# Range checks of the weights at chunk boundaries, LayerNorm's high part straight from x, and sums with high parts first, in a two-layer attention and FFT-filter kernel

## The chip, the cores and the metric

The kernel runs on one core of a Trainium2 chip. Its engines are TensorE (PE; its weight loads are shown apart as PEld), VectorE (DVE), ScalarE (ACT), GpSimd (POOL) and SyncE (SP, which issues most DMAs). The metric is the device time of one execution in microseconds (us); the median of several runs counts.

## The reference

x is 2048 x 1024 in float32; the model has two layers, each an attention with 32 heads of 32 and a filter in the frequency domain, all with the same weights.

```python
def _A_ref(x, wqkv, wo):
    qkv = (x @ wqkv).reshape(B, S, 3, H, Dh).transpose(2, 0, 3, 1, 4)
    q, k, v = qkv[0], qkv[1], qkv[2]
    p = softmax(einsum("bhqd,bhkd->bhqk", q, k) * Dh ** -0.5, axis=-1)
    o = einsum("bhqk,bhkd->bhqd", p, v)
    return o.transpose(0, 2, 1, 3).reshape(B, S, D) @ wo

def _B_ref(x, w_r, w_i):
    X = rfft2(x, axes=(-2, -1)) * (w_r + 1j * w_i)
    return irfft2(X, s=(S, D), axes=(-2, -1))

for _ in range(2):
    x = x + _A_ref(_layernorm(x), wqkv, wo)
    x = x + _B_ref(_layernorm(x), w_r, w_i)
```

## The kernel before

**Numbers as two halves.** A float32 operand of a large matmul is split into a float16 high part and a float16 rest (`split`: ScalarE writes the high part, L167, VectorE the rest, L168), and a product is three matmuls: high by high, high by rest, rest by high. This holds only in a range of values, so the kernel gathers range checks: the largest magnitude of wqkv, of wo and of the filter's weights, the smallest variance and the largest reciprocal of a softmax sum. `combine_flags` makes one number of them at the end (L1126 to L1156), and if it is set, a slower general path computes everything again. With the inputs given it is not set. The weights are the same in both layers, and the maxima are taken in the first one.

**Stages of one layer.**
1. *Head.* `ln` normalises 16 tiles of 128 rows. For a tile, ScalarE writes xn = (x − mean) · r (L315) and then its high part `hl` (L167), VectorE writes the rest, and SP issues two transposing DMAs (L320) that put both parts into the buffer `big`. The sums for V (`v_tiles`, L382) and for q and k (`qk_chunk`, L338) of the first head group follow. ScalarE and VectorE carry each finished sum out of PSUM (`R<-x`, `R<-o`).
2. *Attention loop.* Eight groups `g` of four heads, four chunks `c` of 512 queries, sixteen tiles `kt` of 128 keys. For each (g, c, kt) PE makes scores (`S`, L564), ScalarE exponentials (L568, 128x1024 each, two per tile), PE the products with V (`PV`, L574), and VectorE adds the exponentials up (`add`: the first two tiles in L585, the others in L587) into `acc`. A boundary is the passage from one chunk to the next: 31 in a loop. There `fin` adds `acc` over partitions with four matmuls by ones (the column sums, L593), takes reciprocals (L594 to L599) and scales the output (L600); `out` stores it. Between all this PE works off the q, k and V sums of later groups as filler (q and k sums L338, V sums L382), and `Weights.prep` loads and splits the weights for them, slice by slice of 128x512 (`wst`), three slices ahead.
3. *End of attention:* the product with wo (L440), and the residual.
4. *Filter.* Transposes and a first matmul (32 steps, L795, L804), a loop over 36 steps that works on 32 units (`fb` L864, `fc` L896 and the complex products L903 to L912, `binv` L864, `cinv` L933), then the inverse stage. `loadw` fetches one unit's weights, two units ahead; GpSimd flips signs in them (L848).

**Order of work.** PE and ScalarE follow the order of the code in the attention loop; the other engines, and all of them elsewhere, are ordered by the compiler's scheduler, which places each instruction when it expects it to be ready. Each engine runs its list strictly in order.

**Where the maxima are taken.** In the first layer `Weights.prep` reduces each slice behind its split (L259, 48 in all: 13 in the head, 35 in the loop); `absmax` loads wo a second time and reduces it in 16 pieces in the first filter stage (L789), and `loadw` reduces each unit's weights (L840, 32). L840 stands ahead of L848 and reads the tile that L848 rewrites.

At a chunk boundary the last pair of exponentials is added in two iterations, and `fin` runs in the second, kt = 1:

```python
                for w in late[:1]:
                    add(*w)
                    if w[2] == NKT - 1:
                        fin(*w[:2])
```

Of the kernel before, what the change touches and what calls it, by code (L numbers as in the profile page):

```python
# [115 lines left out]
def ln_scale(nc, sm, cst, mv, eng, n=1):  # L116
# [7 lines left out]
    eng.tensor_tensor(r, r, q, op=ALU.mult)  # L124
    return r
# [63 lines left out]
class AttnPools:  # L189
# [22 lines left out]
    def open_small(self):  # L212
        small = self.small = Pools(self.tc, "left")
        self.pp = small("at_p", 8)
        self.qp = small("at_q", 1)
# [11 lines left out]
class Weights:  # L227


    def __init__(self, nc, ap, wp, flag):  # L230
        self.nc, self.ap, self.wp, self.flag, self.W, self.n = nc, ap, wp, flag, {}, 0

    def prep(self, ph):
# [22 lines left out]
        for i, (h, l, _) in enumerate(sl):  # L256
            split(nc, h, l, st[i], SW)
            if self.flag is not None:
                nc.vector.tensor_reduce(self.flag.pop(), st[i], axis=AX.XY, op=ALU.max, apply_absolute_value=True)  # L259
            load()  # L260
            yield

# [5 lines left out]
def attention(nc, tc, layer, ap, xin, yd, wts, wo, cst, dram, flags):  # L268
# [29 lines left out]
    def ln(t0, n):  # L298
# [10 lines left out]
        r = ln_scale(nc, sm, cst, mv, nc.vector, n)  # L309
        b = sm.tile([128, n], F32, name=f"lb{n}")  # L310
        nc.vector.scalar_tensor_tensor(b, mv[:, 0::2], -1.0, r, op0=ALU.mult, op1=ALU.mult)
        for i in range(n):
            t = t0 + i
            xn = pp.tile([128, 1024], F32, name="xn", tag="p")
            nc.scalar.activation(xn, ap.x[:, t], AF.Identity, bias=b[:, i:i + 1], scale=r[:, i:i + 1])  # L315
            hl = pp.tile([128, 2, 1024], F16, name="hl", tag="p")
# [7 lines left out]
    def qk_chunk(ph, c):  # L324
# [11 lines left out]
        for d in range(8):  # L336
            for i, (a, b) in enumerate(((w[:, 0, d], xh[c][:, d]), (w[:, 0, d], xl[c][:, d]), (w[:, 1, d], xh[c][:, d]))):
                nc.tensor.matmul(ps, a, b, start=d == 0 and i == 0, stop=d == 7 and i == 2)  # L338
                if d < 7 or i < 2:
                    yield  # L340
# [29 lines left out]
    def v_tiles(ph, t2):  # L370
# [6 lines left out]
        for j in range(2):  # L377
            c, o = t2 // 2, (t2 % 2) * 256 + j * 128
            for d in range(8):
                a, b = xh[c][:, d, o:o + 128], xl[c][:, d, o:o + 128]  # L380
                for i, (l, r) in enumerate(((a, w[:, 0, d]), (a, w[:, 1, d]), (b, w[:, 0, d]))):
                    nc.tensor.matmul(ps[:, j], l, r, start=d == 0 and i == 0, stop=d == 7 and i == 2)  # L382
                    if (3 * d + i) % 2 and (j, d, i) != (1, 7, 2):
                        yield
# [165 lines left out]
    last_v = vk.pop()  # L550
    for v in vk:
        run(v)
# [28 lines left out]
    def add(g, c, kt):  # L581
        for hf in range(2):
# [3 lines left out]
            elif kt:  # L586
                nc.vector.tensor_add(acc[hf], acc[hf], p)  # L587
# [46 lines left out]
    with tc.manual_schedule(engines={mybir.EngineType.PE, mybir.EngineType.Activation}):  # L634
        for g in range(NG):
# [3 lines left out]
            for u in range(NCH * NKT):  # L639
# [4 lines left out]
                if kt % 2 == 0:  # L644
# [3 lines left out]
                    pend = []  # L648
                for w in late[:1]:
# [32 lines left out]
        run(wof)  # L682
    with tc.manual_schedule(engines={mybir.EngineType.PE}):
# [72 lines left out]
def spectral(nc, tc, ap, yd, xout, a, cst, fast, flags=None, nxt=None):  # L756
# [23 lines left out]
    wos = []  # L780

    def absmax(i):

        if flags is not None and 0 <= i < 16:
            s = p3.tile([128, 512], F32, name="wo")
            nc.sync.dma_start(s, a["wo"][(i // 2) * 128:(i // 2 + 1) * 128, (i % 2) * 512:(i % 2) * 512 + 512])
            wos.append(s)
        while len(wos) == 3 or (wos and i == 15):
# [453 lines left out]
```

## Time and profile before

| | us |
|---|---|
| median of 3 runs (lowest, highest) | 3838.1 (3837.19, 3840.38) |
| profiled execution, its own time | 3841.8 |
| span of the profiled execution | 3839.8 |

| stage, first layer / second layer | us |
|---|---|
| head, up to the first scores | 118.2 / 152.8 (with the inverse stage of the filter before it) |
| attention loop | 1508.7 / 1489.8 |
| end of attention | 47.8 / 47.9 |
| first filter stage | 49.1 / 48.8 |
| unit loop of the filter | 162.4 / 150.7 |
| inverse stage and stores, second layer | 63.6 |

The profile is of one execution. "Busy" is the time in which an engine executes an instruction; a group is all instructions of one line and shape. In a timeline a row begins with the start in us and a length; `x4` means four instructions in a row, and a bracket at the end tells how long the engine idled before it and what it then got. Names such as `R`, `big` or `wst` are buffers: `R<-R,p` is the sum of exponentials, `Q<-x,Q` the rest of a q sum, `wqk<-wst,wqk` the rest of a weight slice.

### The profile page before, as it was taken

The numbers are of one execution on the slowest core, as the hardware profiler recorded it, in microseconds if no ns is written. First come the engines' busy times: TensorE is split into PE (matmuls) and PEld (weight loads), VectorE is DVE, ScalarE is ACT, GpSimd is POOL, SyncE is SP. The second block draws the span as 40 slices with busy tenths as digits, with TensorE's granted clock in tenths as the row PEclk, the third lists the DMA queues.
The fourth block names the chain that finished last, engine by engine and source line by source line (L and its number), as shares of the span: only waits on it lengthen the run. The fifth ranks groups of instructions, "written<-read, shape, count | busy, mean of one in ns | idle before, by whom it ended". The sixth has DMA issues, their size and how long they took to land.

```text
span 3839.8 us, 79585 instructions
## 1 busy us (share of the span) xinstructions
PE 3713.6 (97%) x32951; PEld 1637.3 (43%) x32951; DVE 3165.3 (82%) x3869; ACT 2900.6 (76%) x3567; POOL 309.1 (8%) x386
## 2 busy tenths in 40 slices
PE   6999999999999999999989999999999999999998
PEld 4422433342234233378854334333423432333788
DVE  6789899889998988965666998899899889889554
ACT  4687887888788876667856888888888888666595
POOL 1000000000000000004320000000000000000143
PEclk9999999999999999999999999999999999999999
DMA  8000000000000221244270000000000002112433
GB/s 206 15 18 18 12 12 18 18 12 16 14 26 7 72 67 70 72 147 135 63 176 15 18 18 13 12 18 23 10 18 12 23 12 91 53 64 72 151 99 105
DMA packets 165573, 194.07 MB, mean 51 GB/s; under 512 B 74960, under 2 KB 120656, under 8 KB 164176
## 3 DMA queue, kind: packets, MB, share of 16 engines
q1 hardware_dynamic: 164912, 188.82, 16.0%
q8 instruction: 260, 4.26, 0.5%
q14 instruction: 113, 0.93, 0.1%
q10 hardware_dynamic: 288, 0.07, 0.0%
HBM read 123.83 MB, written 48.23 MB: 45 GB/s over the span
## 4 chain that ended last, share of the span: by engine, by line
PE 74%; DVE 11%; issue 8%; ACT 3%; DMA 2%; POOL 2%; SPq 0%; DVEq 0%; POOLq 0%; ACTq 0%
PE o L574 20%; PE s L564 17%; PE x L338 12%; PE x L382 7%; PE x L440 6%; DVE R L587 3%; PE s L440 2%; PE ps L864 2%; PE ps L804 2%; ACT p L568 1%; PE s L593 1%; PE ps L795 1%; PE ps L979 1%; DMA wst<-in_wp 1%; PE ps L933 1%
## 5 line engine op out<-in xcount | busy, mean ns | idle before, releaser
L568 ACT ACTIVATE p<-s,bias 128x1024 f32<-128x1024 f32 x2048 | 2169.8, 1112 | 553.6 <-PE s L564 536.7
L587 DVE TENSOR_TENSOR R<-R,p 128x1024 f32<-128x1024 f32 x1792 | 2084.4, 1217 | 109.0 <-ACT p L568 105.7
L574 PE MATMUL o<-p,R 128*32 128x512 f32 x8192 | 985.2, 598 | 0.0
L338 PE MATMUL x<-big,wqk 128*128 128x512 f16 x2880 | 679.2, 381 | 16.8 <-DVE R L168 7.6
L564 PEld LDWEIGHTS <-R 32*128 32x128 f16 x12288 | 231.2, 92 | 755.3 <-issue 639.8
L338 PEld LDWEIGHTS <-wqk 128*128 128x128 f16 x3072 | 276.9, 98 | 449.7 <-issue 163.0
L574 PEld LDWEIGHTS o<-p,R 128*32 128x32 f32 x8192 | 213.7, 109 | 524.1 <-issue 524.1
L564 PE MATMUL s<-R 32*128 32x512 f16 x6144 | 430.2, 378 | 6.7 <-ACT p L568 5.0
L564 PE MATMUL s<-Q,R 32*128 32x512 f16 x6144 | 425.7, 378 | 7.1 <-DVE R L481 5.5
L382 PE MATMUL x<-wv,big 128*128 128x256 f16 x2784 | 331.9, 276 | 35.4 <-DMA big<-hl 35.4
L382 PEld LDWEIGHTS <-big 128*128 128x128 f16 x3072 | 293.1, 99 | 147.3 <-issue 68.9
L585 DVE SCALAR_TENSOR_TENSOR R<-p 128x1024 f32<-128x1024 f32 x128 | 153.8, 1203 | 197.2 <-ACT p L568 196.8
L440 PE MATMUL x<-big 128*128 128x512 f16 x1050 | 241.6, 380 | 0.0
L363 POOL PARTITION_ALL_REDUCE mall<-mqk x16 | 43.0, 2684 | 2310.6 <-DVE mqk L357 2299.1
L440 PEld LDWEIGHTS <-big 128*128 128x128 f16 x1344 | 124.3, 98 | 180.6 <-issue 42.7
L912 DVE TENSOR_TENSOR H<-G,H 128x512 f16<-128x512 f32 (+1 forms) x68 | 46.3, 680 | 113.7 <-ACT H L911 113.6
L864 PE MATMUL ps<-cbi,H 128*128 128x256 f16 (+1 forms) x792 | 100.2, 275 | 7.6 <-ACT H L911 6.0
L857 ACT COPY U<-ps 64x256 f32<-64x256 f32 (+1 forms) x272 | 97.2, 357 | 10.9 <-PE ps L864 5.8
L857 ACT COPY B<-ps 64x256 f32<-64x256 f32 (+1 forms) x272 | 97.1, 357 | 7.0 <-PE ps L864 3.5
L864 PE MATMUL ps<-cb,big 128*128 128x256 f16 x780 | 97.2, 274 | 0.0
L167 ACT ACTIVATE R<-x 128x512 f16<-128x512 f32 x88 | 52.6, 598 | 53.4 <-PE x L338 53.3
L864 PEld LDWEIGHTS <-H 128*128 128x128 f16 (+1 forms) x792 | 76.6, 99 | 20.2 <-ACT H L911 7.1
(428 smaller groups left out, 2922.8 us busy)
## 6 DMA issues: line engine op xcount, KB each, us to landing
wst<-in_wp SPq DMA_DIRECT2D x96, 256.0 KB, 3.0
R<-y SPq DMA_DIRECT2D x32, 512.0 KB, 5.3
w<-in_w SPq DMA_DIRECT2D x60, 256.0 KB, 2.7
od<-ohl SPq DMA_DIRECT2D x56, 256.0 KB, 2.4
big<-od SPq DMA_DIRECT2D x16, 896.0 KB, 6.9
y<-R SPq DMA_DIRECT2D x20, 512.0 KB, 2.6
R<-in_x SPq DMA_DIRECT2D x16, 512.0 KB, 5.5
wst<-in_wo SPq DMA_DIRECT2D x32, 256.0 KB, 3.1
```

The lines of the kernel that those rows point to most:

```text
L167: nc.scalar.activation(hi, src, AF.Copy, scale=scale)
L338: nc.tensor.matmul(ps, a, b, start=d == 0 and i == 0, stop=d == 7 and i == 2)
L382: nc.tensor.matmul(ps[:, j], l, r, start=d == 0 and i == 0, stop=d == 7 and i == 2)
L440: nc.tensor.matmul(p, a, b, start=start and d == ds[0] and i == 0, stop=stop and d == ds[-1] and i == 2)
L564: nc.tensor.matmul(s[h // 2][:, h % 2], K[g][r, a, kt * 128:kt * 128 + 128], Q[g][r, b, c * 512:c * 512 + 512], start=i == 0, stop=i == 2)
L568: nc.scalar.activation(p, s[hf], AF.Exp, bias=bias[g], scale=SCALE / (SQ * SQ))
L574: nc.tensor.matmul(O[g, c][32 * h:32 * h + 32], V[g][:, kt, 32 * h:32 * h + 32], P[g, c, kt, h // 2][:, h % 2], start=kt == 0, stop=kt == ...
L585: nc.vector.scalar_tensor_tensor(acc[hf], P[g, c, 0, hf], 1e-34, p, op0=ALU.add, op1=ALU.add)
L587: nc.vector.tensor_add(acc[hf], acc[hf], p)
L804: nc.tensor.matmul(pa[:, j], tt[:, j], mm[:, g], start=True, stop=True)
L857: nc.scalar.copy(ov[64 * r:64 * r + 64, a0:a0 + m, x], tl[64 * x:64 * x + 64, :m, r])
L864: nc.tensor.matmul(out, l, r, start=k == 0, stop=k == len(mm_) - 1)
```

## The change

1. *Maxima.* The reduces L259, L789 and L840, and the second load of wo in L789's stage, go. A list `unseen` of pieces takes their place, and `look()` takes the maximum of one piece. In the first layer the pieces are the float16 high parts of split weights, 128x1024, 24 in all (five in the head, nineteen at boundaries). In the second layer they are the 17 pieces of the filter's weights and the 8 of wo, 128x1024 float32, loaded into a pool of two buffers one boundary ahead (`take`).
2. *Boundaries.* Both last adds, then `look`, then `fin` stand in iteration kt = 0.
3. *LayerNorm.* ScalarE writes the high part straight from x, with the factor 256 in r; xn is a second activation of x; the rest is a subtraction. The high part's transpose is issued ahead of the rest's.
4. *Sums.* A q, k or V sum takes its 16 matmuls with the high part of x first, then the 8 with the rest.
5. *Flags.* `combine_flags` runs in the unit loop of the second filter, at step 20, with PSUM tiles of that loop; only the load of the result stays at the end.
6. `dynamic_dma_scratch_size=4096` is passed to the compiler.

```diff
@@ Weights
         for i, (h, l, _) in enumerate(sl):
             split(nc, h, l, st[i], SW)
-            if self.flag is not None:
-                nc.vector.tensor_reduce(self.flag.pop(), st[i], axis=AX.XY, op=ALU.max, apply_absolute_value=True)
             load()
             yield
+        if self.flag is not None:
+            v = w[:, 0].rearrange("p d n -> p (d n)")
+            self.unseen += [(v[:, o:o + 1024], None) for o in range(0, 512 * len(sl), 1024)]
+
+    def take(self, i):
+        if len(self.unseen) > i and self.unseen[i][1] is not None:
+            src = self.unseen[i][1]
+            t = self.ap.lookp.tile([128, 1024], F32, name="look")[:, :src.shape[1]]
+            self.nc.sync.dma_start(t, src)
+            self.unseen[i] = (t, None)
+
+    def look(self):
+        if self.unseen:
+            self.take(0)
+            self.nc.vector.tensor_reduce(self.cols.pop(0), self.unseen.pop(0)[0], axis=AX.X, op=ALU.max,
+                                         apply_absolute_value=True)
+            self.take(0)
@@ ln
-            xn = pp.tile([128, 1024], F32, name="xn", tag="p")
-            nc.scalar.activation(xn, ap.x[:, t], AF.Identity, bias=b[:, i:i + 1], scale=r[:, i:i + 1])
             hl = pp.tile([128, 2, 1024], F16, name="hl", tag="p")
-            split(nc, hl[:, 0], hl[:, 1], xn, SX)
+            xn = pp.tile([128, 1024], F32, name="xn", tag="p")
             c, o = t // 4, (t % 4) * 128
-            for j, p in enumerate((xh, xl)):
-                nc.sync.dma_start(p[c][:, :, o:o + 128], hl[:, j], transpose=True)
+            for dst in (hl[:, 0], xn):
+                nc.scalar.activation(dst, ap.x[:, t], AF.Identity, bias=b[:, i:i + 1], scale=r[:, i:i + 1])
+            nc.sync.dma_start(xh[c][:, :, o:o + 128], hl[:, 0], transpose=True)
+            nc.vector.tensor_sub(hl[:, 1], xn, hl[:, 0])
+            nc.sync.dma_start(xl[c][:, :, o:o + 128], hl[:, 1], transpose=True)
@@ qk_chunk (v_tiles alike)
-        for d in range(8):
-            for i, (a, b) in enumerate(((w[:, 0, d], xh[c][:, d]), (w[:, 0, d], xl[c][:, d]), (w[:, 1, d], xh[c][:, d]))):
-                nc.tensor.matmul(ps, a, b, start=d == 0 and i == 0, stop=d == 7 and i == 2)
+        mms = [(w[:, i, d], xh[c][:, d]) for d in range(8) for i in range(2)] + [(w[:, 0, d], xl[c][:, d]) for d in range(8)]
+        for i, (a, b) in enumerate(mms):
+            nc.tensor.matmul(ps, a, b, start=i == 0, stop=i == 23)
@@ attention loop
+                    if kt == 0 and late:
+                        for w in late:
+                            last_add = add(*w)
+                        with tc.issue_after(last_add.ins):
+                            wts.look()
+                        done = [late[1][:2]]
+                        fin(*done[0])
+                        late = []
                 for w in late[:1]:
                     add(*w)
-                    if w[2] == NKT - 1:
-                        fin(*w[:2])
-                        done = [w[:2]]
@@ loadw
-        if flags is not None:
-            nc.vector.tensor_reduce(flags["wb"][:, i:i + 1], wt, axis=AX.X, op=ALU.max, apply_absolute_value=True)
@@ unit loop of the filter
+        if i == 20 and join:
+            join(ps)
@@ build
+        later = [a["w"][:, o:min(o + 1024, WOFF[-1])] for o in range(0, WOFF[-1], 1024)]
+        later += [a["wo"][128 * d:128 * d + 128, :] for d in range(8)]
```

How the engines' lists change is seen at three places. VectorE at the second boundary of the first layer, before; `zt<-s` reads the column sums, the two L585 begin the new chunk:

```order
L587 TENSOR_TENSOR R<-R,p 128x1024 x4
L585 SCALAR_TENSOR_TENSOR R<-p 128x1024
L594 STREAM_TRANSPOSE zt<-s 128x512
L585 SCALAR_TENSOR_TENSOR R<-p 128x1024
L596 RECIPROCAL rc<-zt 128x16
L597 TENSOR_TENSOR fr<-fr,rc 128x16
L599 STREAM_TRANSPOSE zt<-rc 128x512
L168 SCALAR_TENSOR_TENSOR Q<-x,Q 128x512
L600 SCALAR_TENSOR_TENSOR zt<-oc,zt 128x512
```

And after, at the same place (L613 is the old L587, L611 the old L585, L171 the old L168):

```order
L613 TENSOR_TENSOR R<-R,p 128x1024 x4
L281 TENSOR_REDUCE fw<-wqk 128x1
L621 STREAM_TRANSPOSE zt<-s 128x512
L623 RECIPROCAL rc<-zt 128x16
L624 TENSOR_TENSOR fr<-fr,rc 128x16
L626 STREAM_TRANSPOSE zt<-rc 128x512
L627 SCALAR_TENSOR_TENSOR zt<-oc,zt 128x512
L611 SCALAR_TENSOR_TENSOR R<-p 128x1024 x2
L171 SCALAR_TENSOR_TENSOR Q<-x,Q 128x512
```

PE at the same boundary, before and then after (L593 and L620 are the column sums, L564 and L590 scores, L600 the product with V, L338 filler; LDWEIGHTS loads a matmul's weights):

```order
L564 LDWEIGHTS R
L564 MATMUL s<-R 128x512
L593 MATMUL s<-R,ones 32x512 x4
L338 LDWEIGHTS wqk
L338 MATMUL x<-big,wqk 128x512
```

```order
L600 MATMUL o<-p,R 32x512 x8
L620 MATMUL s<-R,ones 32x512 x4
L590 LDWEIGHTS R
L590 MATMUL s<-R 128x512
L590 LDWEIGHTS R
```

The column sums have moved from behind the scores of kt = 1 to ahead of them. On VectorE the look stands behind the last add, and all of `fin` ahead of the first adds of the new chunk. Eight rows further on before, two reduces `fw<-wst` of the weight slices stood between the adds; they are gone. VectorE in the unit loop of the first filter, one unit before and after:

```order
L903 TENSOR_TENSOR G<-ps,w 128x256
L840 TENSOR_REDUCE fwb<-w 128x1
L904 TENSOR_TENSOR t__20768<-ps,w 128x256
L905 TENSOR_TENSOR G<-ps,w 128x256
L906 TENSOR_TENSOR t__20768<-ps,w 128x256
L912 TENSOR_TENSOR H<-G,H 128x2x256
```

```order
L922 TENSOR_TENSOR G<-ps,w 128x256
L923 TENSOR_TENSOR t__20609<-ps,w 128x256
L924 TENSOR_TENSOR G<-ps,w 128x256
L925 TENSOR_TENSOR t__20609<-ps,w 128x256
L931 TENSOR_TENSOR H<-G,H 128x2x256
```

Only the reduce is missing. ScalarE in the first head around the first sums of k and q, before; `R<-x` and `R<-o` carry them out of PSUM, the rest is LayerNorm:

```order
L167 ACTIVATE R_90<-x_471 128x512
L315 ACTIVATE xn_456<-R_90,lb2_454,r2_446 128x1024
L167 ACTIVATE hl_458<-xn_456 128x1024
L315 ACTIVATE xn_463<-R_90,lb2_454,r2_446 128x1024
L167 ACTIVATE hl_465<-xn_463 128x1024
L315 ACTIVATE xn_518<-R_90,lb2_516,r2_508 128x1024
L167 ACTIVATE R_90<-o_533 128x512
```

And after:

```order
L170 ACTIVATE R_92<-x_468 128x512
L340 ACTIVATE hl_453<-R_92,lb2_451,r2_443 128x1024
L340 ACTIVATE xn_454<-R_92,lb2_451,r2_443 128x1024
L340 ACTIVATE hl_460<-R_92,lb2_451,r2_443 128x1024
L340 ACTIVATE xn_461<-R_92,lb2_451,r2_443 128x1024
L340 ACTIVATE hl_515<-R_92,lb2_513,r2_505 128x1024
L340 ACTIVATE xn_516<-R_92,lb2_513,r2_505 128x1024
L340 ACTIVATE hl_522<-R_92,lb2_513,r2_505 128x1024
L340 ACTIVATE xn_523<-R_92,lb2_513,r2_505 128x1024
L170 ACTIVATE R_92<-o_530 128x512
```

The high part now comes ahead of xn, and the second sum's evacuation (`R<-o`) has eight activations of LayerNorm ahead of it instead of five.

More of the change, by code (lines that the diff above doesn't have):

```diff
@@ L550, in attention @@
     last_v = vk.pop()
+    if layer == 0:
+        for _ in range(5):
+            wts.look()
     for v in vk:
@@ L682, in attention @@
         run(wof)
+    assert not wts.unseen and not wts.cols
     with tc.manual_schedule(engines={mybir.EngineType.PE}):
@@ L779, in spectral @@
     xo = ap.x.rearrange("p t (a u g q) -> p g a t u q", a=8, g=2, q=8)
[L780 to L788, printed above, removed]
-            tc.keep_in_program_order(nc.vector.tensor_reduce(flags["wcol"].pop(), wos.pop(0), axis=AX.X, op=ALU.max, apply_absolute_value=True))
     def t1(i):
```

86 lines of the change are left out of this document (45 added, 41 removed).

## The prediction

> **What bounds the kernel now.** I read the page first, then the windows view cut at the stage borders, then the groups and the timeline inside the stages that differ.
>
> ```profile
> PE 3713.6 (97%) x32951; PEld 1637.3 (43%) x32951; DVE 3165.3 (82%) x3869; ACT 2900.6 (76%) x3567; POOL 309.1 (8%) x386
> ```
>
> TensorE (PE) is busy for 97% of the span and the change neither adds nor takes out a matmul of weight. So what can be won is PE's idle time, 3839.8 − 3713.6 = 126 us, and PE time that runs at a lower clock. The windows view says where it lies (columns: window, its length, busy us of the engines with their instructions, granted clock, DMA share, GB/s).
>
> ```profile
> core 0: us, PE busy (x) PEld busy (x) DVE busy (x) ACT busy (x) POOL busy (x), PEclk, DMA share, GB/s
> 0.00:118.20 118.20, 86.09 (x536) 53.56 (x537) 67.70 (x160) 50.52 (x63) 17.15 (x22) 0.96 0.71 172
> 118.20:1626.90 1508.70, 1485.33 (x13666) 515.52 (x13666) 1351.05 (x1429) 1183.87 (x1248) 33.36 (x31) 1.00 0.09 29
> ...
> 1723.80:1886.20 162.40, 152.63 (x1303) 136.19 (x1303) 94.76 (x231) 132.31 (x340) 70.44 (x102) 0.99 0.34 106
> 1886.20:1951.30 65.10, 49.48 (x393) 48.39 (x392) 56.66 (x113) 37.64 (x62) 23.47 (x11) 0.93 0.29 100
> 1951.30:2039.00 87.70, 82.12 (x536) 52.69 (x536) 38.38 (x82) 39.24 (x50) 14.56 (x14) 0.96 0.73 159
> 2039.00:3528.80 1489.80, 1478.42 (x13665) 513.63 (x13664) 1328.32 (x1394) 1183.93 (x1248) 35.41 (x31) 1.00 0.09 29
> ...
> 3625.50:3776.20 150.70, 147.05 (x1302) 134.19 (x1302) 74.44 (x190) 130.41 (x340) 70.12 (x102) 1.00 0.36 113
> ```
>
> The program runs the same pair of stages twice, and the second pass is a ready-made experiment: the weight maxima are taken in the first pass only. The attention loop takes 1508.7 us with them and 1489.8 without (18.9 less), the filter's unit loop 162.4 and 150.7 (11.7 less). PE does the same matmuls in both. DVE has 1429 − 1394 = 35 instructions more in the first attention loop.
>
> ```profile
> L259 DVE TENSOR_REDUCE fw<-wst 128x1 f32<-128x512 f32 x35 | 23.5, 684 | 8.6 <-DMA wst<-in_wp 7.8
> ```
>
> Those 35 are exactly the reduces of the weight slices (count, busy us, mean ns, idle before). PE's own groups show how they reach it: first the first attention loop, then the second.
>
> ```profile
> L338 PE MATMUL x<-big,wqk 128*128 128x512 f16 x1344 | 318.3, 382 | 9.4 <-DVE Q L168 6.2 <-DVE R L168 3.2
> L593 PE MATMUL s<-R,ones 128*32 128x512 f32 x248 | 37.2, 604 | 2.2 <-DVE R L587 2.2
> ```
>
> ```profile
> L338 PE MATMUL x<-big,wqk 128*128 128x512 f16 x1344 | 316.8, 380 | 0.2
> L593 PE MATMUL s<-R,ones 128*32 128x512 f32 x248 | 33.0, 605 | 0.0
> ```
>
> With the reduces, the q and k sums (L338) wait 9.4 us for DVE's splits of the sum before, and the column sums (L593) 2.2 us for late adds; without, 0.2 and 0. DVE is a queue in order: a 0.68 us reduce, or its wait for a weight slice (8.6 us idle), delays the split behind it.
>
> **The change part by part**, against the profiled execution: 3841.8 us, of which 3839.8 is the span and 2.0 lies around it.
>
> *First attention loop.* The 35 reduces go; 19 looks (reduces of 1024 fp16 high parts) come at chunk boundaries. What lies there is in the timeline of one boundary, and in the group of the first adds of all chunks, second pass:
>
> ```profile
> 204.54 4.62 DVE L587 TENSOR_TENSOR R<-R,p 128x1024 f32<-128x1024 f32 x4
> 208.74 1.92 PE L574 MATMUL o<-p,R 128*32 128x512 f32 x16
> 210.60 0.83 PE L564 MATMUL s<-R 32*128 32x512 f16 x12
> 211.35 1.06 PE L593 MATMUL s<-R,ones 128*32 128x512 f32 x8
> ...
> 212.61 1.23 DVE L585 SCALAR_TENSOR_TENSOR R<-p 128x1024 f32<-128x1024 f32 x1 [3.44 <-ACT p L568]
> 213.75 0.71 DVE L594 STREAM_TRANSPOSE zt<-s 128x512 f32<-128x512 f32 x1
> ```
>
> ```profile
> L585 DVE SCALAR_TENSOR_TENSOR R<-p 128x1024 f32<-128x1024 f32 x64 | 76.9, 1203 | 103.3 <-ACT p L568 103.3
> ```
>
> DVE idles 3.44 us there, until ScalarE has the first exponentials of the new chunk; over the loop it is 103.3 us, 103.3/31 = 3.3 per boundary. No look stands in the trace. Its price lies between that of L259 (0.68, half as many elements) and 2 × 0.68 = 1.36; I take 1.2, the 1.217 us of an add over the same 128x1024. 1.2 fits in 3.3. DVE's total work in this loop then hardly changes (−23.5 + 19 × 1.2 = −0.7 us), only its place. I take **−18**, the difference of the two passes less one, with −20 to −12 as bounds: the lower gain is what PE's summed idle shows, 1508.7 − 1485.33 = 23.4 against 1489.8 − 1478.42 = 11.4.
>
> The column sums move too: PE now does its four at once behind the chunk's last product with V, ahead of the next scores. They need the last add. Above, the add ends at 204.54 + 4.62 = 209.16 and the product at 208.74 + 1.92 = 210.66, so nothing waits: 0. PE has the same work; ScalarE gets the next scores 1.06 us later, and DVE's idle time grows by as much. The chain behind it (transpose 0.71, reciprocal, transpose, product, about 2.5 us) then falls into the rest of the idle time, together with the look: 1.2 + 2.5 = 3.7 against 3.3 + 1.06 = 4.4. Cover just suffices.
>
> By the Trainium skill ("VectorE: DVE Perf Modes", "The perf-mode tier table (the rule you actually need)") tensor_reduce has the 1× rate for every type, so fp16 gains nothing by its width; the rows can't test it, since all reduces here read fp32. By it the sum stands; if fp16 ran twice as fast, 24 looks would take some 0.5 us less each, inside idle time, and the sum would stand as well.
>
> *First filter.* 32 reduces of the filter's weights (L840) leave the unit loop, 16 of wo with their loads leave the stage ahead of it. The chain of waits in the first pass's loop:
>
> ```profile
> 1852.31 0.60 DVE fwb L840
> 1852.98 0.30 POOL w L848
> 1853.67 0.73 POOL G L907
> ...
> 1856.99 0.60 DVE fwb L840
> ```
>
> The reduce sits on the chain, since GpSimd's L848 rewrites the slice that it reads: 1856.99 − 1852.31 = 4.68 us for a unit. In the second pass the same chain is PE alone:
>
> ```profile
> 3756.91 1.31 PE ps L864 x12
> 3758.22 0.89 PE ps L933 x8
> 3759.11 1.31 PE ps L864 x12
> 3760.42 0.89 PE ps L896 x8
> ```
>
> that is 1.31 + 0.89 + 1.31 + 0.89 = 4.40 a unit. 162.4 − 150.7 = 11.7: **−12**, bounds −13 and −9 (32 units × 0.28).
>
> *First head.* Thirteen of the reduces stand here, before the loop.
>
> ```profile
> 57.43 5.34 PE L338 MATMUL o<-big,wqk 128*128 128x512 f16 x24 [1.85 <-DVE R L168]
> ```
>
> ```profile
> 77.34 0.69 DVE L259 TENSOR_REDUCE fw<-wst 128x1 f32<-128x512 f32 x1 [4.49 <-DMA wst<-in_wp]
> 77.94 0.68 DVE L168 SCALAR_TENSOR_TENSOR R<-x,R 128x512 f16<-128x512 f32 x1
> 78.68 6.70 PE L338 MATMUL x<-big,wqk 128*128 128x512 f16 x24 [4.35 <-DVE R L168]
> ```
>
> At 77.34 DVE waits 4.49 us for a slice, the split of a finished sum stands behind it, and PE waits 4.35; its next sum takes 6.70 instead of 5.34, 1.36 more. From the window's clock this is the throttle:
>
> ```profile
> 75.00:80.00 5.00, 1.32 (x4) 0.48 (x4) 1.95 (x3) 0.03 (x1) 0.00 (x0) 0.80 0.93 210
> ```
>
> The granted clock is 0.80 there. By the Trainium skill ("TensorE: Matmul & The Clock Gate", "Part 1: The HAM clock gate (the "warmup" mystery)") an idle window of about 3.4 us halves the clock; the row agrees, and by that rule the 1.36 goes with the wait. Without reduces, wait and slow sum go: 4.35 + 1.36 = 5.7. The high part comes one activation earlier, since ScalarE writes it straight from x,
>
> ```profile
> 14.41 1.06 ACT L167 ACTIVATE hl<-xn 128x1024 f16<-128x1024 f32 x1
> ```
>
> and the sums take all high parts first. Each is worth a microsecond where PE waits for a transpose. Against it: DMA is at a share of 0.93 around 78 us, so a transfer may only take the reduce's place as the last, and ScalarE's order now puts an evacuation of a q sum behind several normalisations, of 1.06 to 1.23 us each. I take **−5**, bounds −12 (5.7, the 1.85 at 57.43 and a few transposes) and +3 (nothing won, three activations late).
>
> *Second head.* The first V sum waits for the transposes of fresh high parts:
>
> ```profile
> 1951.29 0.61 PE L382 MATMUL x<-wv,big 128*128 128x256 f16 x2 [13.35 <-DMA big<-hl]
> ```
>
> They now start one activation earlier: **−1**, bounds −4 and +2.
>
> *Second attention loop.* It had no reduce; it gets 25 looks over fp32, 25 × 1.2 = 30 us of DVE, 1328.3 to 1358 in 1489.8, and 25 loads of 512 KB at a DMA share of 0.09, each asked for a whole chunk (48 us) ahead on SyncE's queue, behind which stand later weight loads. Cover: 31 × 3.3 = 102 us of idle time at the very places. **+1**, bounds −2 (waits of the column sums that vanish) and +6 (0.25 us at each of 25 looks).
>
> *Flags.* A dozen small DVE operations, a transpose and a one-column matmul move from the tail into the second filter's loop, where PE is the bound: **+1**, bounds 0.3 and 3 (a small PE pair, then a stall while a PSUM buffer of the loop is held). In the tail, the conversion ended at 3829.01 + 0.14, but SyncE waits for the last output anyway:
>
> ```profile
> 3829.01 0.14 DVE L1155 CAST fi<-fb 1x1 int32<-1x1 f32 x1
> ```
>
> ```profile
> SPq L1204 <- SPq L1204: 5.2, 1, 5.2
> ```
>
> So **0** there, bounds −1.3 and 0. The smaller scratch for dynamic DMAs and the folded scale SX cost nothing visible: 0.
>
> Sum: −18 − 12 − 5 − 1 + 1 + 1 + 0 = −34, 3841.8 − 34 = 3807.8. The median of the runs is 3838.1, 3.7 below the profiled execution; on it the sum gives **3804**.
>
> **Rivals.**
> (a) *The head gains nothing*: another transfer is late where the reduce was. For: DMA share 0.93. Against: the dense sums behind 80 us need only what had come. Then −29: 3809.
> (b) *The filter loop keeps its period*, as products on DVE or GpSimd take the reduce's place. For: the chain also holds L907. Against: the second pass runs the same products in 150.7. Then −22: 3816.
> (c) *DVE's load counts, not the place* (no gain, at worst slower): the change adds DVE work, 24 × 1.2 + 25 × 1.2 = 59 us against 80 reduces of attention and filter at 0.68 = 54 us, and the second loop alone gets 30. In the first pass 23.5 us of reduces cost 18.9, 0.80 per us; then the first loop gains 0, the second loses 30 × 0.80 = 24: −5 − 12 − 1 + 24 + 1 = +7, 3845; at 1.36 a look +10, 3848. For: that price. Against: the reduces of before stood amid the adds and waited for DMA, the looks stand in idle time.
> (d) *The early column sums stall PE*, slower: all of the 62 boundaries now have the sums ahead of the next scores, so a late last add holds up scores, exponentials and adds. The point where this eats the gain is 34/62 = 0.55 us a boundary; at 1.2 (DVE one add late) it costs 74: +40, 3878. For: in the first pass one boundary shows such a wait,
>
> ```profile
> 718.40 2.09 PE L593 MATMUL s<-R,ones 128*32 128x512 f32 x8 [1.73 <-DVE R L587]
> ```
>
> but it came with the reduces ahead of the adds. Against: the 0.0 of the second pass.
>
> **How the numbers follow.** Forecast 0.65, (a) 0.10, (b) 0.06, (c) 0.09, (d) 0.05; 0.05 for half of (c) in the second loop, 3816. A measurement tells 0.2% (7.7 us) from no change. Faster: all but (c) and (d), 0.86. (c) splits, 0.06 the same and 0.03 slower (looks at 1.36); with (d) slower is 0.08. The bounds of the terms summed are −52 and +4, which seldom come together; the range from 3788 to 3824 holds the forecast with one or two terms at their ends, (a), (b) and half of (c).
>
> **What would show it.** Right: the first attention loop near 1490 us, L338's wait for DVE gone; the unit loop near 151 in both passes; the second loop within some us of 1490; looks of about 1.2 us between the last add and the first of the next chunk; the first head some 5 us shorter with no 4 us wait near 77. Wrong: column sums that wait for adds at many boundaries (d), a second loop longer by 10 to 25 us (c), a head as long as before (a), L907's wait in place of L840's (b).

## The result and the profile after

| | before | after |
|---|---|---|
| median of 4 runs (lowest to highest), us | 3839.03 (3837.19 to 3840.38) | 3795.84 (3794.53 to 3796.20) |
| ratio, 95% interval | | 0.9887 (0.987 to 0.9904) |
| profiled execution / its span, us | 3841.8 / 3839.8 | 3796.2 / 3794.4 |

The change saves 43.2 us, where 34 were forecast. The page's first part and the windows view of the changed kernel, cut at the same instructions as before (columns as there; new names: L613 the adds, L611 a chunk's first adds, L620 the column sums, L590 the scores, L361 and L405 the q/k and V sums, L171 the splits of finished sums, L365 and L378 their squares and norms, L281 the looks):

```profile
PE 3699.0 (97%) x32951; PEld 1642.0 (43%) x32951; DVE 3180.3 (84%) x3824; ACT 2898.8 (76%) x3567; POOL 308.1 (8%) x386
```

```profile
core 0: us, PE busy (x) PEld busy (x) DVE busy (x) ACT busy (x) POOL busy (x), PEclk, DMA share, GB/s
0.00:117.63 117.63, 86.16 (x537) 53.85 (x539) 65.00 (x152) 51.81 (x63) 15.21 (x22) 0.94 0.73 173
117.63:1602.21 1484.58, 1475.85 (x13666) 517.22 (x13665) 1359.78 (x1414) 1182.49 (x1248) 34.44 (x31) 1.00 0.08 29
...
1699.04:1852.74 153.70, 148.68 (x1302) 134.66 (x1300) 74.86 (x190) 130.82 (x340) 70.37 (x102) 1.00 0.36 117
1852.74:1914.13 61.39, 48.92 (x393) 48.19 (x391) 52.71 (x107) 35.92 (x62) 23.68 (x11) 0.94 0.28 100
1914.13:2000.41 86.28, 83.09 (x536) 52.66 (x537) 40.38 (x88) 42.06 (x51) 14.60 (x14) 0.97 0.75 167
2000.41:3484.58 1484.17, 1475.48 (x13666) 516.98 (x13665) 1366.66 (x1426) 1182.69 (x1248) 34.97 (x31) 1.00 0.11 37
...
3582.15:3734.47 152.32, 147.98 (x1305) 134.60 (x1303) 75.17 (x193) 130.29 (x340) 70.23 (x102) 1.00 0.34 112
3734.47:3794.40 59.93, 48.70 (x392) 48.12 (x390) 31.64 (x54) 28.58 (x50) 21.36 (x7) 0.94 0.50 143
```

DVE has become busier (3180.3 after 3165.3) and the kernel faster. Against the forecast by stage, from these rows and those of before (whose unit loop, with borders read to 0.01 us, is 162.34 us, its inverse stage and second head 152.85):

| stage | forecast | measured |
|---|---|---|
| first head | −5 | −0.6 |
| first attention loop | −18 | −24.1 |
| first filter, unit loop | −12 | −8.6 |
| inverse stage and second head (152.8 before) | −1 | −5.2 |
| second attention loop | +1 | −5.6 |
| second filter: its first stage and unit loop | +1 | +2.5 |
| last inverse stage and tail | 0 | −3.7 |

The sum is −45.3 of the 45.4 between the spans; no other stage moved by more than 0.2. Two things are as predicted in kind. First, L361's waits in the first loop are gone (9.4 us before); the groups of PE there:

```profile
L361 PE MATMUL x<-big,wqk 128*128 128x512 f16 x1344 | 316.8, 380 | 0.3 <-DVE Q L171 0.2
...
L620 PE MATMUL s<-R,ones 128*32 128x512 f32 x248 | 33.4, 594 | 1.4 <-DVE R L504 1.4
```

Second, the price of a look. The view of its line (ns shortest/median/longest, then first and last start) gives 1.21 us, and the same for float16 and float32. The Trainium skill ("VectorE: DVE Perf Modes", "The perf-mode tier table (the rule you actually need)") gives tensor_reduce the 1× rate alone, and these rows agree:

```profile
L281 DVE TENSOR_REDUCE fwb<-look x17: 406/1212/1214, 2048.1 to 2764.5; 128x1 f32<-128x1024 f32 x16, 128x1 f32<-128x256 f32 x1
L281 DVE TENSOR_REDUCE fw<-wqk x16: 1159/1210/1215, 28.2 to 1285.1; 128x1 f32<-128x1024 f16 x16
```

### The profile page after: what moved, and what is told of

Same layout as the page of the kernel before. It is cut to its first block, busy times and chain, and to the rows that moved or that the text cites. A ratio compares the mean times of both kernels' runs of the same rounds, so it can differ in the third digit from the quotient of the medians.

```text
span 3794.4 us, 79594 instructions
## 1 busy us (share of the span) xinstructions
PE 3699.0 (97%) x32951; PEld 1642.0 (43%) x32951; DVE 3180.3 (84%) x3824; ACT 2898.8 (76%) x3567; POOL 308.1 (8%) x386
## 4 chain that ended last, share of the span: by engine, by line
## 5 line engine op out<-in xcount | busy, mean ns | idle before, releaser
L613 DVE TENSOR_TENSOR R<-R,p 128x1024 f32<-128x1024 f32 x1792 | 2087.2, 1218 | 130.7 <-ACT p L594 127.4
L600 PE MATMUL o<-p,R 128*32 128x512 f32 x8192 | 984.9, 598 | 0.0
L361 PE MATMUL x<-big,wqk 128*128 128x512 f16 x2880 | 676.9, 380 | 1.9 <-ACT R L409 1.5
L590 PEld LDWEIGHTS <-R 32*128 32x128 f16 x12288 | 230.6, 92 | 753.4 <-issue 637.4
L361 PEld LDWEIGHTS <-wqk 128*128 128x128 f16 x3072 | 276.0, 98 | 425.9 <-issue 138.8
L600 PEld LDWEIGHTS o<-p,R 128*32 128x32 f32 x8192 | 213.7, 109 | 523.4 <-issue 523.4
L590 PE MATMUL s<-R 32*128 32x512 f16 x6144 | 429.5, 377 | 6.3 <-DVE mqk L380 3.4
L590 PE MATMUL s<-Q,R 32*128 32x512 f16 x6144 | 427.3, 377 | 4.6 <-DVE R L504 2.6
L405 PE MATMUL x<-wv,big 128*128 128x256 f16 x2784 | 331.3, 275 | 30.2 <-DMA big<-hl 30.2
L405 PEld LDWEIGHTS <-big 128*128 128x128 f16 x3072 | 293.0, 99 | 132.8 <-issue 57.3
L611 DVE SCALAR_TENSOR_TENSOR R<-p 128x1024 f32<-128x1024 f32 x128 | 150.7, 1217 | 34.1 <-ACT p L594 34.1
L931 DVE TENSOR_TENSOR H<-G,H 128x512 f16<-128x512 f32 (+1 forms) x68 | 47.1, 693 | 118.3 <-ACT H L930 118.1
L621 DVE STREAM_TRANSPOSE zt<-s 128x512 f32<-128x512 f32 x64 | 45.7, 715 | 62.8 <-PE s L620 62.6
L832 DVE TENSOR_TENSOR big<-ps,big 128x512 f16<-128x512 f32 x64 | 44.5, 695 | 58.1 <-ACT big L831 58.1
```

The costliest lines, as they stand in the source:

```text
L361: nc.tensor.matmul(ps, a, b, start=i == 0, stop=i == 23)
L405: nc.tensor.matmul(ps[:, j], l, r, start=i == 0, stop=i == 23)
L590: nc.tensor.matmul(s[h // 2][:, h % 2], K[g][r, a, kt * 128:kt * 128 + 128], Q[g][r, b, c * 512:c * 512 + 512], start=i == 0, stop=i == 2)
L600: nc.tensor.matmul(O[g, c][32 * h:32 * h + 32], V[g][:, kt, 32 * h:32 * h + 32], P[g, c, kt, h // 2][:, h % 2], start=kt == 0, stop=kt == ...
L611: nc.vector.scalar_tensor_tensor(acc[hf], P[g, c, 0, hf], 1e-34, p, op0=ALU.add, op1=ALU.add)
L613: last_add = nc.vector.tensor_add(acc[hf], acc[hf], p)
```

## The experiments

Stage times in us, each from the windows of one profile. The changed kernel was run three times (a_again and a_again2 are its repeats), so its rows show the spread. Between kernels that share the code of a stage the spread can be wider (unit loop 1 without reduces: 151.5 to 155.0; inverse stage and second head with the new LayerNorm: 146.5 to 150.2).

| kernel | first head | loop 1 | unit loop 1 | inverse + head 2 | loop 2 | unit loop 2 | tail | ratio to before (95%) |
|---|---|---|---|---|---|---|---|---|
| before | 118.2 | 1508.7 | 162.3 | 152.8 | 1489.8 | 150.7 | 63.6 | 1 |
| changed | 117.6 | 1484.6 | 153.7 | 147.7 | 1484.2 | 152.3 | 59.9 | 0.9887 (0.987, 0.9904) |
| a_again | 119.7 | 1485.2 | 152.9 | 147.4 | 1486.5 | 153.7 | 59.9 | 0.9878 (0.9861, 0.9894) |
| a_again2 | 118.4 | 1485.0 | 153.2 | 147.7 | 1486.1 | 153.0 | 59.8 | 0.9867 (0.985, 0.9883) |
| b_noreduce | 110.8 | 1489.3 | 152.0 | 151.8 | 1491.1 | 151.0 | | |
| a_nolook | 114.4 | 1485.7 | 153.0 | 150.2 | 1484.4 | 151.0 | | |
| a_finlate | 119.6 | 1489.4 | 155.0 | 146.5 | 1489.3 | 153.6 | 59.6 | 0.9891 (0.9875, 0.9908) |
| a_flagend | 119.0 | 1485.0 | 152.2 | 147.9 | 1484.1 | 153.1 | 61.8 | 0.987 (0.9854, 0.9887) |
| a_ln | 113.1 | 1485.0 | 152.4 | 149.9 | 1484.6 | 151.7 | 59.8 | 0.9869 (0.9853, 0.9885) |
| a_sumorder | 118.1 | 1484.9 | 152.3 | 147.8 | 1485.8 | 151.7 | 59.8 | 0.9872 (0.9856, 0.9889) |
| a_lookmid | 117.2 | 1493.9 | 151.9 | 148.1 | 1498.8 | 152.8 | 60.4 | 0.9944 (0.9928, 0.9961) |
| a_look2 | 115.8 | 1487.5 | 153.1 | 146.7 | 1492.8 | 151.6 | 59.9 | |
| b_finearly | 120.6 | 1507.1 | 161.9 | 152.1 | 1485.7 | 151.3 | 63.4 | |
| best | 108.8 | 1486.1 | 151.5 | 147.1 | 1484.3 | 152.9 | 59.9 | 0.9847 (0.9831, 0.9863) |

**What the reduces cost** (b_noreduce): before, without any maximum.

```diff
@@ Weights.prep
-            if self.flag is not None:
-                nc.vector.tensor_reduce(self.flag.pop(), st[i], axis=AX.XY, op=ALU.max, apply_absolute_value=True)
@@ first filter stage
-        if i % 2:
-            absmax(i // 2)
@@ loadw
-        if flags is not None:
-            nc.vector.tensor_reduce(flags["wb"][:, i:i + 1], wt, axis=AX.X, op=ALU.max, apply_absolute_value=True)
```

> The kernel before, with all its maxima of weights left out (no reduces of slices, of wo or of the filter's weights, no second load of wo), and nothing else changed. If the reduces' place in VectorE's queue is what cost the time, the first attention loop comes to 1489 to 1491 us (1508.7 before), the unit loop of the first filter to 151 (162.4), the first head loses its 4.35 us wait and is 113 to 118; whole 3839 - 30 = 3803 to 3810. Rival, other parts of the change brought the first loop's gain: the first loop stays above 1500 and the whole above 3820.

The windows of its first head, first loop, first unit loop and second loop:

```profile
0.00:110.75 110.75, 83.84 (x537) 52.66 (x539) 60.24 (x155) 49.39 (x63) 15.64 (x22) 0.98 0.79 184
110.75:1600.01 1489.26, 1478.72 (x13665) 513.54 (x13665) 1328.29 (x1394) 1182.98 (x1248) 33.96 (x31) 1.00 0.09 29
1697.58:1849.59 152.01, 147.59 (x1303) 134.30 (x1300) 75.47 (x190) 130.44 (x340) 69.84 (x102) 1.00 0.35 112
2001.39:3492.45 1491.06, 1479.81 (x13665) 514.02 (x13665) 1328.45 (x1394) 1183.04 (x1248) 30.25 (x31) 1.00 0.09 29
```

The maxima are zero here, which sets the flag for too small weights, and the general path runs behind the fast one (30989 us in all); this and the next kernel are read by their stages alone. The first loop comes within 2 us of the second, as expected: its 35 reduces cost 19.4 us, those of the unit loop 10.3, and those of the head 7.4 (up to 10 against b_finearly, whose head has the same code and took 120.6), which is more than the 5.7 that were read from one wait.

**What the looks cost** (a_nolook): the changed kernel without them.

```diff
-        if self.unseen:
+        if False:
```

> The changed kernel with no looks at all: the maxima and their 25 loads are left out. If the looks lie wholly in idle time, both attention loops stay at 1484 us (1483.5 to 1485) and the whole within 2 us of 3796. Rival, VectorE's load counts: 19 and 25 looks of 1.21 us give back 0.80 us for each us, the first loop falls by 18 and the second by 24, the whole to about 3754.

The windows of its two loops:

```profile
114.36:1600.04 1485.68, 1477.41 (x13665) 517.41 (x13665) 1338.27 (x1394) 1181.79 (x1248) 33.97 (x31) 1.00 0.09 29
2000.40:3484.80 1484.40, 1475.64 (x13666) 517.09 (x13665) 1338.16 (x1394) 1181.60 (x1248) 34.17 (x31) 1.00 0.09 29
```

The loops stay, though DVE's busy time falls by 21.5 and 28.5 us. At the boundaries the looks are free. In the head, leaving five looks out gains 3 to 5 us: 114.4 against 117.6 to 119.7. That is no price per look, though: with each look done twice (a_look2 below) the head takes 115.8.

**Place or load** (a_lookmid, a_look2): the same looks amid a chunk, and each look twice at the boundary.

```diff
-                        with tc.issue_after(last_add.ins):
-                            wts.look()
...
                 for w in late[:1]:
-                    add(*w)
+                    last_add = add(*w)
+                    if kt == 8 and g + c:
+                        with tc.issue_after(last_add.ins):
+                            wts.look()
```

> The changed kernel with the same looks amid a chunk (behind the add in the iteration kt = 8) and no longer at the boundary. If the place decides, as predicted, 19 looks of 1.21 us cost up to 18 us in the first loop and 25 cost up to 24 in the second, by the 0.80 us per us that the old reduces cost: loops 1495 to 1502 and 1500 to 1508, the whole 3820 to 3838. If VectorE only has to have the time somewhere in a chunk (it idles 4 us in each), the loops stay at 1484 to 1487 and the whole within 5 us of the changed kernel; then the old reduces cost so much for their waits on loads or for where the scheduler put them, right ahead of splits.

Against the middle of the three controls (1485.0 and 1486.1) the loops grow by 8.9 and 12.8 us, for 23 and 30 us of looks: some 0.4 us per us, just short of the ranges expected. The whole is 0.9944 of before, where the control beside it was 0.9878. The place decides, though at half the price of the old reduces; what doubled theirs, the wait for a load or the place right ahead of a split, was not tested apart. The second loop's PE groups, of the changed kernel and then with looks amid the chunk:

```profile
L620 PE MATMUL s<-R,ones 128*32 128x512 f32 x248 | 33.4, 594 | 1.4 <-DVE R L504 1.4
...
L378 PE MATMUL s<-sq,bones 128*32 128x512 bf16 x56 | 6.7, 388 | 1.6 <-DVE sq L365 1.2 <-ACT p L594 0.2
```

```profile
L361 PE MATMUL x<-big,wqk 128*128 128x512 f16 x1344 | 316.8, 380 | 2.5 <-DVE Q L171 2.3
...
L620 PE MATMUL s<-R,ones 128*32 128x512 f32 x248 | 37.8, 594 | 1.4 <-DVE R L504 1.4
...
L378 PE MATMUL s<-sq,bones 128*32 128x512 bf16 x56 | 8.2, 387 | 6.6 <-DVE sq L365 6.2 <-ACT p L594 0.2
```

The old symptom is there again: sums wait for splits (2.3), norms for squares (6.2), and the column sums spread from 33.4 to 37.8 us, as before's first loop had 37.2 against 33.0.

```diff
-            self.nc.vector.tensor_reduce(self.cols.pop(0), self.unseen.pop(0)[0], axis=AX.X, op=ALU.max,
-                                         apply_absolute_value=True)
+            col, src = self.cols.pop(0), self.unseen.pop(0)[0]
+            for _ in range(2):
+                self.nc.vector.tensor_reduce(col, src, axis=AX.X, op=ALU.max, apply_absolute_value=True)
```

> The changed kernel with each look done twice, 24 and 25 more reduces of 1.21 us. Behind a look VectorE still idles 1.29 us until the column sums are there. If idle time at the boundary covers it, both loops stay at 1484 to 1487. If load counts as it did amid the chunk (0.40 to 0.47 us per us), they come to 1493 and 1498.

Between the two, in one profile: +2.5 in the first loop (1487.5), +6.7 in the second (1492.8). The cover holds one look and most of a second. In the second loop the q and k sums wait 5.2 us in all, at six places, for a split that stands behind a doubled look; in the first they wait 0.7 us, at one. Why the second loop has more such places was not found.

**The early column sums** (a_finlate, b_finearly): the changed kernel with the old boundary, and the old kernel with the new one.

```diff
-                    if kt == 0 and late:
-                        for w in late:
-                            last_add = add(*w)
...
                 for w in late[:1]:
-                    add(*w)
+                    last_add = add(*w)
+                    if w[2] == NKT - 1:
+                        with tc.issue_after(last_add.ins):
+                            wts.look()
+                        fin(*w[:2])
+                        done = [w[:2]]
```

> The changed kernel with the late adds, the look and the column sums put back: one add per iteration, look and column sums in the iteration kt = 1. If the early column sums brought the 5 us that both attention loops gained beyond the reduces, both loops come to 1489 to 1491 and the whole to 3805 to 3808. If the order of the sums or nothing of this brought it, the loops stay at 1484 to 1486 and the whole at 3796 to 3799. If the look now delays the first adds of a chunk, the loops go past 1495.

Both loops come to 1489.3 to 1489.4: against 1484.6 to 1485.2 and 1484.2 to 1486.5 with the early sums, this move is the 3 to 5 us that both loops gained beyond the reduces. The timeline of one boundary, first loop; the changed kernel:

```profile
203.63 4.62 DVE L613 TENSOR_TENSOR R<-R,p 128x1024 f32<-128x1024 f32 x4
...
207.82 1.92 PE L600 MATMUL o<-p,R 128*32 128x512 f32 x16
...
208.17 1.21 DVE L281 TENSOR_REDUCE fw<-wqk 128x1 f32<-128x1024 f16 x1
209.57 1.04 PE L620 MATMUL s<-R,ones 128*32 128x512 f32 x8
...
210.54 0.83 PE L590 MATMUL s<-R 32*128 32x512 f16 x12
210.68 0.72 DVE L621 STREAM_TRANSPOSE zt<-s 128x512 f32<-128x512 f32 x1 [1.29 <-PE s L620]
211.30 2.76 PE L361 MATMUL x<-big,wqk 128*128 128x512 f16 x12
...
214.00 0.83 PE L590 MATMUL s<-R 32*128 32x512 f16 x12
```

and with the old order:

```profile
210.17 1.92 PE L600 MATMUL o<-p,R 128*32 128x512 f32 x16
...
212.02 0.83 PE L590 MATMUL s<-R 32*128 32x512 f16 x12
...
212.78 1.06 PE L620 MATMUL s<-R,ones 128*32 128x512 f32 x8
...
213.78 2.76 PE L361 MATMUL x<-big,wqk 128*128 128x512 f16 x12
...
216.47 0.83 PE L590 MATMUL s<-R 32*128 32x512 f16 x12
```

PE waits for nothing in either stretch, and does the same instructions: from the product with V to the second scores 214.00 − 207.82 = 6.18 us against 216.47 − 210.17 = 6.30. Of the 0.12, 0.10 lies at the product with V: what follows it starts 1.75 us after it where that is the column sums (209.57 − 207.82), and 1.85 us where it is scores (212.02 − 210.17). Read in the same way, 20 of the first loop's 31 boundaries are shorter by 0.12 to 0.15 us, three by 0.26 (a wait of 0.2 for exponentials goes there as well), and eight are as long as before: 3.4 us together. The first loop of a_finlate as a whole:

```profile
119.63:1608.98 1489.35, 1478.32 (x13665) 513.38 (x13665) 1349.97 (x1414) 1183.38 (x1248) 34.34 (x31) 1.00 0.09 29
```

Beside 1484.58 and 1475.85 of the changed kernel, PE is busy for 2.5 us less and idle for 2.3 us less (11.0 to 8.7). So about half of the gain is the tighter order and half are shorter waits, those of the norms (L378) above all: 3.0 us with the old order, 1.6 with the new. The look, too, fits as worked out: it ends at 209.38, and DVE still idles 1.29 us.

> The kernel before with one part of the change alone: both late adds and the column sums in the iteration kt = 0; all reduces stay where they were. If the early column sums bring their 5 us on their own, the second loop falls from 1489.8 to 1484 to 1486. In the first loop, which keeps its reduces, 1503 to 1505 if the gains add up; above 1508.7 if late adds now hold up the scores at the boundary, as the fourth rival of the prediction has it.

Alone, the move gives the second loop its 4.1 us (1485.7), but the first, with its reduces, only 1.6. The column sums wait 2.7 us for late adds there, after 2.2 before: the fourth rival's mechanism is there, far too small to turn the sign, and too small to explain all that is missing.

**The head** (a_ln, a_sumorder): LayerNorm as before, and the sums interleaved as before, each in the changed kernel.

```diff
-            for dst in (hl[:, 0], xn):
-                nc.scalar.activation(dst, ap.x[:, t], AF.Identity, bias=b[:, i:i + 1], scale=r[:, i:i + 1])
...
-            nc.vector.tensor_sub(hl[:, 1], xn, hl[:, 0])
+            nc.scalar.activation(xn, ap.x[:, t], AF.Identity, bias=b[:, i:i + 1], scale=r[:, i:i + 1])
+            split(nc, hl[:, 0], hl[:, 1], xn, SX)
```

> The changed kernel with LayerNorm written as before (xn first, the high part from xn, both transposes behind the split). If writing the high part straight from x is what shortened the stretch from the first filter's inverse stage to the second loop (152.9 to 147.7 us), that stretch comes back to 151 to 153; if the order of the sums did it, it stays at 147 to 149. If the new LayerNorm is also what gave back the gain in the first head, that head falls from 118 to 111 to 115; if the five looks did it alone, it stays at 117 to 119.

The first head falls to 113.1. So in this kernel the new LayerNorm costs it 5 to 7 us (117.6 to 119.7 with it). The changed kernel's timeline of ScalarE, then of PE:

```profile
48.26 1.24 ACT L340 ACTIVATE hl<-R,lb,r 128x1024 f16<-128x1024 f32 x1 [3.20 <-DVE lb L333]
...
56.20 1.23 ACT L340 ACTIVATE xn<-R,lb,r 128x1024 f32<-128x1024 f32 x1
57.34 0.58 ACT L170 ACTIVATE R<-o 128x512 f16<-128x512 f32 x1
```

```profile
44.21 5.34 PE L361 MATMUL o<-big,wqk 128*128 128x512 f16 x24
...
59.08 0.38 PE L378 MATMUL s<-sq,bones 128*32 128x512 bf16 x1 [3.98 <-POOL sq L365]
...
63.37 6.92 PE L361 MATMUL o<-big,wqk 128*128 128x512 f16 x24 [2.85 <-DVE R L171]
```

The sum ends at 49.55; eight activations from 48.26 on keep its evacuation until 57.34. GpSimd's square and PE's norm wait for it (3.98), the next use of its bank waits for the rest (2.85), and the sum behind that takes 6.92 us instead of 5.34: the granted clock is 0.50 from 60 to 66 us and 1.00 from 67 us on. With the old LayerNorm (line numbers one lower) ScalarE and PE go on at once, and one wait of 3.49 us is left, near 70 us:

```profile
45.22 5.34 PE L360 MATMUL o<-big,wqk 128*128 128x512 f16 x24
50.40 5.40 PE L404 MATMUL x<-wv,big 128*128 128x256 f16 x48
55.64 5.34 PE L360 MATMUL o<-big,wqk 128*128 128x512 f16 x24
```

```profile
50.60 0.60 ACT L170 ACTIVATE R<-o 128x512 f16<-128x512 f32 x1
```

The late evacuation is not LayerNorm's doing alone, though. The seven profiles with the new LayerNorm and five looks in the head all show it, with PE waits of 3.0 to 5.7 us for that square. In a_nolook and a_look2, which have the new LayerNorm too, the compiler chose another order, and the waits are others (1.27 and 3.63 us; 1.35 and 4.47 us).

The stretch of inverse stage and second head goes from 147.7 to 149.9: there the new LayerNorm gains 2.2 of the 5.2 us, of which 1.3 in the first V sum's wait for transposes (11.73 us, 13.02 in a_ln, 13.35 before). Of the other 3.0, 1.2 are a wait of the inverse stage's matmuls for VectorE, 1.6 us before, 0.4 in the changed kernel and 0.3 in a_ln. In a_nolook it is 1.6 again, and the stretch takes 150.2. The code of that stage is the same in all of them; why the wait comes and goes was not found.

> The changed kernel with the q, k and V sums interleaved as before (high, rest, high for each of 8 steps). Attention loops unchanged at 1484 to 1485 under every theory, since no sum waits for a transpose there. If the order of the sums shortened the second head, the stretch from the inverse stage to the second loop goes from 147.7 to 151 to 153; if LayerNorm did, it stays at 147 to 149. First head: 113 to 116 if the new order cost there, 117 to 119 if not.

Nothing moves beyond the spread of the controls (second stretch 147.8, head 118.1). The order of the sums is worth nothing here.

**The flags** (a_flagend): joined at the end again.

```diff
-                spectral(nc, tc, ap, y, x, a, cst, True, join=lambda ps: combine_flags(nc, ps, cp, flags, cst))
+                spectral(nc, tc, ap, y, x, a, cst, True)
...
+        with tc.tile_pool(name="flag_ps", bufs=1, space=PSUM) as ps:
+            combine_flags(nc, ps, cp, flags, cst)
```

> The changed kernel with the flags joined at the end again, as before. As predicted (the tail hides the flag chain behind the last output): the second unit loop falls from 152.3 to 150.7, the tail stays at 59.9, the whole comes to 3794. Rival, the flag chain and the load of its result are on the path at the end: the tail goes from 59.9 back to 63.6, the loop gives 1.7 of it, the whole comes to 3798.

The tail grows by 1.9 (61.8), the unit loop, at 153.1, falls by nothing: the join costs nothing that the spread lets one see, and the chain at the end was on the path. In the medians this does not show (0.987 for this kernel). The DMA view of the last 14 us (GB/s in 40 slices of about 0.35 us), before and then after:

```profile
GB/s 290 288 291 291 291 287 288 255 313 288 288 244 295 288 285 285 294 279 271 234 119 47 0 0 0 0 0 0 0 23 47 70 0 0 0 0 0 0 0 0
```

```profile
GB/s 289 293 289 289 192 0 46 0 0 46 38 284 270 276 292 287 294 293 280 253 310 292 333 265 267 272 292 296 311 294 292 114 46 23 34 0 0 0 0 0
```

Before, the output is out in slice 22, nothing moves for 2.5 us, then a few small transfers come and the program ends; after, the small transfers lie partly ahead of the last output and partly right behind it. Before, all that moves from 3836.4 us on is five packets of the queues that the profile calls instruction queues. That they hold the code behind the branch, and wait for the flag, was only argued.

**The mended kernel** (best):

```diff
@@ ln, first layer only
+                xn = pp.tile([128, 1024], F32, name="xn", tag="p")
+                nc.scalar.activation(xn, ap.x[:, t], AF.Identity, bias=b[:, i:i + 1], scale=r[:, i:i + 1])
+                hl = pp.tile([128, 2, 1024], F16, name="hl", tag="p")
+                split(nc, hl[:, 0], hl[:, 1], xn, SX)
...
@@ attention, build
-    if layer == 0:
-        for _ in range(5):
-            wts.look()
+        later += [a["wp"][g, k] for g, k in ((0, 0), (0, 1), (0, 2), (1, 2))]
```

> The changed kernel with two parts mended: the first layer's LayerNorm as before (the second layer keeps the high part straight from x), and no look in the first head; the four maxima of the first group's weights are taken from the float32 weights at boundaries of the second layer, which has six without a look. If the first head's loss comes from these two parts, that head falls from 117.6 to 119.7 to 110 to 112 and everything else stays: the whole 5 to 8 us below the changed kernel. Rival, the head is limited by its transfers and only what the looks cost comes back: 113 to 115, the whole 3 to 4 us below.

> The changed kernel itself, once more, to stand beside the three others on one chip: stage times as in its first profile, first head 117 to 120 us, both attention loops 1484 to 1485, unit loops 152 to 154, and the whole within 5 us of 3796.

> The changed kernel again, beside the mended one on one chip: 3795 to 3799, first head 117 to 120.

The repeats are as expected but for small misses: a_again's loops (1485.2 and 1486.5, expected 1484 to 1485) and a_again2's median (3794.2, expected 3795 to 3799). In the mended kernel the first head is 108.8, some 10 us less and below the 110 to 112 expected, and the whole 3786.9 us (3785.25 to 3787.04) beside 3794.2 (3793.59 to 3798.87) of the changed kernel on the same chip: 7.3 us less, and 0.9847 of before.

## Why the prediction was right, and where it was not

**First attention loop, −18: right in mechanism, short in size.** The reduces alone are −19.4 (b_noreduce), the looks cost nothing (a_nolook); the other 4 to 5 are the early column sums (a_finlate).

**Column sums, "0": this step failed.** It asked only whether they wait. They don't wait for adds: the 1.4 us in the row of L620 lie at one boundary, are for another result of VectorE (L504), and stand at the scores in the old order. But their place in PE's order is itself worth 3 to 5 us in a loop (a_finlate), half by tighter order and half by shorter waits elsewhere, and so the second loop's "+1" became −5.6. The bound of −2 there was too narrow.

**The looks' cover, 4.4 against 3.7 us: right** for one look per boundary; a second one exceeds it (a_look2).

**First filter, −12: too large.** The loop without reduces takes 151.5 to 155.0 in these kernels, and 150.7 to 153.7 in the second layer; the second pass's 150.7 was the low end: −8.6 measured, −10.3 by the reduces alone.

**First head, −5: this step failed.** The reduces alone were worth 7.4, more than the 5.7 in the sum. What the sum named as the risk, ScalarE's order, gave back 5 to 7, and five looks in the head 3 to 5, which the sum did not price at all; the mended kernel wins both back. The two are not separate prices, as the compiler's order changes with each (a_look2). The first rival gives this stage's result (nothing gained) with another cause: not a late transfer but a late evacuation.

**Second head, −1: too small.** LayerNorm gives 2.2, the order of the sums nothing. Of the other 3.0, 1.2 lie in a wait of the inverse stage that comes and goes with the looks (a_nolook); the cause stays open.

**Tail, "0": this step failed.** It took SyncE's 5.2 us wait to hide the flag chain. The chain costs 1.9 (a_flagend); the other 1.8 of the 3.7 were not told apart (the smaller DMA scratch, for one, was not tried alone).

**Flags in the loop, +1:** not visible; the unit loop of the second layer varies by 2.7 us (151.0 to 153.7) between kernels that share its code. The load rival falls: the loops do not mind 21 to 28 us of DVE work at the boundary, and mind it amid the chunk.

The errors of the terms, from +4.4 to −6.6, partly cancelled, which is luck, and the rest lies on the side of the gain: 43 instead of 34. Two of the prediction's sums are off without bearing on this: the upper bounds of the terms add up to −7, not +4, and rival (c) at 1.36 us a look leaves out some 2 us of the first loop.

## What to carry to other kernels

Price a side task by the place where it stands in an in-order queue, not by its length: the same 1.21 us reduce was free in a queue's natural gap, cost 0.4 us per us amid a chunk, and a reduce that could wait for a load ahead of a critical split cost 0.8. Where two passes of the same loop differ in one thing, their difference is a good estimate of it: 18.9 us against 19.4 measured for the attention loop, 11.7 against 10.3 for the unit loop. And when an edit changes what one engine does first, look at the order of all that this engine owes to others: here, in the first head, eight activations ahead of one evacuation cost more than the earlier transpose gained. The compiler may order a stage anew after an edit elsewhere, so a difference of 2 to 4 us in such a stage needs its waits read before it is given to the edit.

## What the hardware showed that was not expected

The same matmuls of PE, with no wait in either order, took 6.18 or 6.30 us by their order alone, and 20 of 31 boundaries show 0.12 to 0.15 us of this kind. A maximum over 1024 elements takes 1.21 us for float16 as for float32. After an idle time of 3.98 us the granted clock fell to 0.50; it stayed there through a second one of 2.85 us, and PE's next sum of 24 matmuls took 6.92 us instead of 5.34. In b_finearly an idle time of 2.38 us was enough (0.50 from 58 to 61 us, 6.83 us for the sum), while 1.85 us at the same place in the kernel before was not (5.34 us).
